# Seven block products in place of eight for two pairs of token-layer chunks, and an older setup in place of a halved one

## The chip, the cores and the metric

The kernel runs on one core of a Trainium2 chip. A core has a TensorE (PE, matrix products; PEld is its weight load), a VectorE (DVE), a ScalarE (ACT), a GpSimd (POOL) and a SyncE (SP, which here only issues transfers); they run side by side and wait for one another at semaphores. Products land in PSUM, eight banks of 128 partitions by 512 float32; everything else lives in SBUF. The metric is the device time of one execution in microseconds (us). Each instruction has one of these engines, and each engine works through its own list in the order in which the program issued it: an instruction that waits holds up all that stand behind it on its engine.

## The reference, cut to what matters

For each of 8 batches a 3008 x 256 input goes through a two-dimensional Fourier transform, of which the real part x is kept, and then through an MLP mixer block: a token layer across the 3008 positions and a channel layer across the 256 channels.

```python
X = np.fft.fft(x, axis=1)
x = np.fft.fft(X, axis=2).real

xt = x.transpose(0, 2, 1)                       # batch, 256, 3008
h = np.maximum(xt @ w_tok1, 0.0) @ w_tok2       # 3008 -> 256 -> 3008
u = x + h.transpose(0, 2, 1)
h2 = np.maximum(u @ w_ch1, 0.0) @ w_ch2         # 256 -> 1536 -> 256
return u + h2
```

The step that the change is about is the second token product, `max(.., 0) @ w_tok2`, and the sum with x that follows it.

## The kernel before

A batch is computed in six chunks of 512 positions (the last has 448 of its own). A chunk is computed in four steps, so that a batch has 24 steps, s0 to s23. A step does a quarter of the first channel product of its chunk (`mm1`, six matmuls of 512 columns into three banks `pc`, each emptied by ACT), a quarter of the second channel product of the chunk before it (`mm2`), and between these it takes pieces from generators that prepare the next batch. The channel product is itself computed with block sums on VectorE (`block_sums`, tiles `sb` and `c`), seven products for eight.

```python
for b in range(BB):
    nxt = front(b + 1) if b + 1 < BB else iter(())
    if b != 1:
        folds = fold(b + 2, [nc.vector] * 4) if b + 2 < BB else None
    for c in range(NCH):
        ...
        for s in range(4):
            sub = 4 * c + s
            n = plan[b][sub]
            mm1(b, c, c1, range(3 * s, 3 * s + 3))
            ...                                    # now(): half of the block sums
            take(own, own_plan[b][sub])            # the rest of this batch's front
            first = 0 if s % 2 else n // 2
            take(nxt, first)                       # pieces of the next batch's front
            ...
            if prev is not None:
                mm2(*prev, s, pbox)
            ...
            take(nxt, n - first)
            ...
            if folds is not None:
                take(folds, fold_plan[b][sub])     # pieces of the fold of batch b + 2
            ...
            if b and sub == 22 and b + 3 < BB:
                x_tiles[b + 3] = load_x(b + 3)     # one buffer: waits for the fold's end
```

`load_x` brings a batch's input (`xp` by four plain transfers, `xm` by two gathers, all issued by GpSimd) into single buffers. `fold` adds the mirrored rows of `xm` to `xp` on VectorE (a mirror piece) and then forms sums and differences of columns in `eo` (two more pieces), four times:

```python
for s, (t0, t1) in enumerate(((13, 17), (9, 13), (5, 9), (1, 5))):
    ...
    if s == 0:
        tt(out=xp[:, 1:NR, 0], in0=xp[:, 1:NR, 0], in1=xm[0:KR, ::-1, 0], op=add)
        tt(out=eo[:, :, 0], in0=xp[:, :, 0], in1=xp[:, :, 0], op=add)
    tt(out=xp[:, t, 1:D], in0=xp[:, t, 1:D], in1=xm[0:KR, rv, D - 1:0:-1], op=add)
    yield
    ...                                            # eo sums; yield; eo differences; yield
fold_plan = [[0] * 8 + [1, 2, 0, 0] * 4 for _ in range(BB)]      # from s8 on
```

`front(b)` makes the transform of a batch (tiles `z`, `w`), the first token product (`pt`), the upper half of x (`third(c)`: `pq` and `py` into PSUM, `yt` on VectorE) and then, chunk by chunk, the second token product with the sum:

```python
def third(c, then=None):
    py, pq = ps_f("py"), ps_f("pq")
    ...                                            # 4 + 4 matmuls of 128 columns
    nc.scalar.activation(out=qs[:], in_=pq[:], func=AFT.Copy)
    ...
    for h, op in ((0, AT.subtract), (1, AT.add)):
        nc.vector.tensor_tensor(out=yt[:, h, CW * c:CW * c + CW], in0=py[:],
                                in1=qs[:], op=op)
...
for c in range(NCH):
    ...
    for h in range(2):
        minus = c >= 3
        pu = ps_f("pu")
        for th in range(2):
            nc.tensor.matmul(pu[:, 0:n], lhsT=uu[:, th, int(minus), h, :],
                             rhs=w2_cols(b, c)[:, th], start=(th == 0), stop=(th == 1))
        ...
        nc.vector.tensor_tensor(out=ut[:, h, 0:n]..., in0=pu[:, 0:n]..., in1=y..., op=AT.add)
        ...
        yield
```

So a chunk takes four matmuls of 512 columns and two adds of 128 x 512 on VectorE. The three banks `ps_f` rotate among `pz`, `pw`, `pt1`, `py`, `pq` and `pu`.

Setup builds tables from angles. Its middle part works in two halves of the groups, so that ScalarE may start on the first half while VectorE makes the second:

```python
for g in halves:
    nc.vector.scalar_tensor_tensor(out=mp[:, g], ...)
for g in halves:
    for i, scale, bias in ((mp, 1.0 / S, up), (vp, 1.0, down)):
        nc.scalar.activation(out=vp[:, g], in_=i[:, g], func=AFT.Identity, ...)
rest_of(halves[0])
...
for g in halves:
    table3(tp, vp, g)
...
warm(12)
pts_p = turn_in(tp, ps_mm)
turned_out(tts_p, pts_p, (0,))
angles_z()
turned_out(tts_p, pts_p, (1,))
table_q()
...
```

Of the kernel before, what the change touches and what calls it, by code (L numbers as in the profile page):

```python
# [10 lines left out]
FP16 = mybir.dt.float16  # L11
# [9 lines left out]
P = 128  # L21
# [20 lines left out]
def kernel(  # L42
# [30 lines left out]
    def ps_f(name, dt=FP32, n=512):  # L73
        return psum.tile([P, n], dt, tag="f", name=name, bufs=3)
# [6 lines left out]
    def ps_any(name, dt=FP32, n=512):  # L81
        tag, bufs = next(r for r in ring if r[0] not in held)
        return psum.tile([P, n], dt, tag=tag, name=name, bufs=bufs)
# [103 lines left out]
    ts(eq32[:], scol[:], 32.0, AT.is_equal)  # L187
    nc.vector.scalar_tensor_tensor(out=reff[:], in0=gt32[:], scalar=-32.0, in1=scol[:],
# [58 lines left out]
    def table3(tab, r, g, shift=(0.0, 0.0)):  # L247
        for i in range(2):
            nc.scalar.activation(out=tab[:, g, 64 * i:64 * i + 64], in_=r[:, g],
                                 func=AFT.Sin, scale=half[i][:], bias=shift[i])  # L250
# [16 lines left out]
    def turned_out(tts, pts, hs=(0, 1)):  # L267
        for h in hs:
            copy(0, tts[0][:, 768 * h:768 * h + 768], pts[h][:, 0:768])
# [46 lines left out]
    halves = slice(0, NG // 2), slice(NG // 2, NG)  # L316
    for g in halves:
        nc.vector.scalar_tensor_tensor(
            out=mp[:, g], in0=jrow[:, 0:64].unsqueeze(1).to_broadcast([P, NG // 2, 64]),
            scalar=r47[:], in1=gp[:, g].unsqueeze(2).to_broadcast([P, NG // 2, 64]),  # L320
            op0=AT.mult, op1=AT.add)
    ts(mid[:], scol[:], 32.0, AT.is_lt)
    ts(tmp[:], scol[:], 1.0, AT.is_ge)
    nc.vector.tensor_tensor(out=mid[:], in0=mid[:], in1=tmp[:], op=AT.mult)
# [4 lines left out]
    for g in halves:  # L329
        for i, scale, bias in ((mp, 1.0 / S, up), (vp, 1.0, down)):  # L330
            nc.scalar.activation(out=vp[:, g], in_=i[:, g], func=AFT.Identity,  # L331
                                 scale=scale, bias=bias[:])

    def rest_of(g):
        nc.vector.scalar_tensor_tensor(out=vp[:, g], in0=vp[:, g], scalar=-float(S),
                                       in1=mp[:, g], op0=AT.mult, op1=AT.add)

    rest_of(halves[0])
# [3 lines left out]
    rest_of(halves[1])  # L342
    ident = const.tile([P, P], FP16, tag="ident")
    ts(ident[:], jrow[:, 0:P], pcol[:], AT.is_equal)
# [6 lines left out]
    for g in halves:  # L351
        table3(tp, vp, g)
    anti = const.tile([P, P], FP16, tag="anti")
    acol = pvec("acol")

    def table_q():
        for g in halves:
            nc.vector.scalar_tensor_tensor(out=vq[:, g], in0=vp[:, g], scalar=side[:],
                                           in1=vp[:, g], op0=AT.mult, op1=AT.max)
        for g in halves:  # L360
            table3(tq, vq, g, (shift0[:], shift1[:]))

    def table_anti():
        ts(acol[:], pcol[:], -1.0, AT.mult, 127.0, AT.add)
        ts(anti[:], jrow[:, 0:P], acol[:], AT.is_equal)

    mask0, mask0h, q24 = (pvec(n) for n in ("mask0", "mask0h", "q24"))
    t1n = const.tile([KR, 2, 2, 24], FP16, tag="t1n")
    t1b = const.tile([KR, 3, 24], FP16, tag="t1b")
    m1 = gen.tile([KR, 5, 24], FP32, tag="m1")  # L370
    cs, v1 = (gen.tile([KR, 5, 24], FP32, tag=n, name=n) for n in ("cs", "v1"))
    t0h = gen.tile([KR, 2, 24], FP16, tag="t0h")

    def angles_z():
        ts(mask0h[:], xicol[:], -0.5, AT.mult, 0.5, AT.add)
        ts(q24[:], qcol[:], 24.0, AT.add)
        for a, n, col, off in ((0, 2, qcol, 47 / 4), (2, 2, qcol, 0.0),
                               (4, 1, q24, 47 / 8)):
            ts(m1[:, a:a + n, :], jrow[0:KR, 0:24].unsqueeze(1).to_broadcast([KR, n, 24]),
               col[0:KR, :], AT.mult, off, AT.add)  # L380
        reduced(v1[:], m1[:], m1[:], 47)
        sin(cs[:], m1[:], 47)
        nc.scalar.activation(out=t0h[:], in_=cs[:, 0:4:2, :], func=AFT.Copy,
                             scale=mask0h[0:KR, :])

    def table_z():
        ts(mask0[:], mask0h[:], 2.0, AT.mult)
        for i, m in ((0, mask0), (1, xicol)):
            ts(t1n[:, :, i, :], cs[:, i:4:2, :], m[0:KR, :], AT.mult)
        ts(t1b[:, 1, :], cs[:, 4, :], float(np.sqrt(0.5)), AT.mult,  # L390
           xicol[0:KR, :], AT.mult)
        nc.vector.tensor_copy(out=t1b[:, 0:3:2, :], in_=t1n[:, :, 0, :])

    nyq = const.tile([KR, P], FP16, tag="nyq")
    ixc = const.tile([P, 1], I32, tag="ixc")

    def rows_c():
        iota(ixc[:], [[0, 1]], D, -1)
        pl.memset(ixc[0:1, :], P)
        load_wc()  # L400

    def angles_d():
        nc.vector.scalar_tensor_tensor(out=md[:], in0=vd[:], scalar=-256.0, in1=md[:],
                                       op0=AT.mult, op1=AT.add)

    td0 = const.tile([P, 131], FP16, tag="td0")
    td1 = const.tile([P, P], FP16, tag="td1")
    alt = const.tile([P, 131], FP16, tag="alt")

# [57 lines left out]

    state = {}

    def fold(b, engs):  # L470
# [4 lines left out]
        for s, (t0, t1) in enumerate(((13, 17), (9, 13), (5, 9), (1, 5))):  # L475
            tt = engs[s].tensor_tensor
            t = slice(t0, t1)
            rv = slice(16 - t0, 16 - t1 if t1 < 17 else None, -1)
            if s == 0:
                tt(out=xp[:, 1:NR, 0], in0=xp[:, 1:NR, 0], in1=xm[0:KR, ::-1, 0], op=add)  # L480
                tt(out=eo[:, :, 0], in0=xp[:, :, 0], in1=xp[:, :, 0], op=add)
            tt(out=xp[:, t, 1:D], in0=xp[:, t, 1:D], in1=xm[0:KR, rv, D - 1:0:-1], op=add)
            yield
            if t0 == 1:
                t = slice(0, t1)
            tt(out=eo[:, t, 1:129], in0=xp[:, t, 1:129], in1=xp[:, t, 255:127:-1], op=add)
            if t0 == 1:
                nc.vector.tensor_copy(out=nyq[:, 0:1], in_=eo[:, 0, P:P + 1])
                nc.vector.memset(eo[:, 0, P:P + 1], 0.0)
            yield  # L490
            tt(out=eo[:, t, 129:256], in0=xp[:, t, 1:128], in1=xp[:, t, 255:128:-1],
               op=sub)
            yield
# [92 lines left out]
    Z0_ORDER = ((11, (0, 1)), (0, (1, 1)), (6, (0, 1)), (1, (0, 1)))  # L586
# [37 lines left out]
    def rest(b):  # L624
# [11 lines left out]
        def part_q(pt):  # L636
            sq = perb.tile([P, 127], FP32, tag="sq", name="sq", bufs=2)
            nc.scalar.activation(out=sq[:], in_=pt[:, 130:257], func=AFT.Copy)
            return sq

        def units(pt, sq):
            uv = perb.tile([P, 2, P], FP32, tag="uv", name="uv", bufs=2)
            nc.vector.tensor_copy(out=uv[:, :, 0], in_=pt[:, 0:130:129])
            nc.vector.tensor_tensor(out=uv[:, 0, 1:P], in0=pt[:, 2:129], in1=sq[:],
                                    op=AT.subtract)
            nc.vector.tensor_tensor(out=uv[:, 1, 1:P], in0=pt[:, 2:129], in1=sq[:],
                                    op=AT.add)
# [11 lines left out]
        def third(c, then=None):  # L659
            py, pq = ps_f("py"), ps_f("pq")  # L660
# [5 lines left out]
            qs = perb.tile([P, CW], FP32, tag="qs", name="qs", bufs=2)  # L666
# [21 lines left out]
        else:  # L688
# [3 lines left out]
            for th in range(2):  # L692
                pt = ps_mm("pt1")
                tok1(pt, th, 0)
                sp = perb.tile([P, 130], FP32, tag="sp", name="sp", bufs=2)
# [17 lines left out]
        uts = st["ut"] = []  # L713
        for c in range(NCH):
            if c in (1, 2):
# [4 lines left out]
            ut = perb.tile([P, 2, CW], FP16, tag="ut", name="ut", bufs=4)  # L720
# [4 lines left out]
            uts.append(ut)  # L725
# [19 lines left out]
            for h in range(2):  # L745
# [6 lines left out]
                if minus:  # L752
                    hi = 2 * HALF - 1 - f0
                    y = yt[:, 1 - h, hi:hi - n:-1]
                else:
                    y = yt[:, h, f0:f0 + n]
# [3 lines left out]
                    in1=y.rearrange("p (a b) -> p a b", b=64), op=AT.add)  # L760
# [192 lines left out]
    warm(12)  # L953
    held.add("o2")
    pts_p = turn_in(tp, ps_mm)
    turned_out(tts_p, pts_p, (0,))
    angles_z()
    turned_out(tts_p, pts_p, (1,))
    table_q()
    table_anti()  # L960
    table_z()
    filler(6)
    turn_rows(tts_p, 1.0, 0)
    filler(10)
    pts_q = turn_in(tq, ps_out)
    filler(4)
    rows_c()
    pieces = fold0()
    take(pieces, 2)
    angles_d()  # L970
    take(pieces, 3)
    own = zw0()
    take(own, 2)
    turned_out(tts_q, pts_q, (0,))
    take(own, 3)
    turned_out(tts_q, pts_q, (1,))
    held.clear()
    take(own, 3)
    table_d()
    table_b()  # L980
    carried(tts_p, hp, 0, 0)
    carried(tts_p, hp, 1, 1)
    turn_rows(tts_q, -1.0, 0)
    carried(tts_p, hp, 2, 1)
    table_perm()
    take(own, 7)
# [18 lines left out]
    for c in range(2, NCH):  # L1005
        for th in range(2):
# [7 lines left out]
    plan = [[0] * 10 + [2] * 10 + [1, 2, 2, 3]] + [[1] * 14 + [2, 1] * 4 + [1, 1]] * (BB - 1)  # L1014
    own_plan = [[2, 1, 1, 1, 1, 1, 1, 0, 1, 1, 0, 0, 1, 1] + [0] * 10,
                [0, 1, 1, 0, 1, 1, 1, 0, 1, 1, 0, 0, 1, 1] + [0] * 10]
    own_plan += [[1, 1, 1, 0, 0, 1, 1, 0, 1, 1, 0, 0, 1, 1] + [0] * 10] * (BB - 2)
    early_plan = [0] * 4 + [2, 2, 1, 2, 1, 2, 2] + [0] * 13
    fold_plan = [[0] * 8 + [1, 2, 0, 0] * 4 for _ in range(BB)]
# [5 lines left out]
    for b in range(BB):  # L1025
# [3 lines left out]
        for c in range(NCH):  # L1029
# [6 lines left out]
            for s in range(4):  # L1036
                sub = 4 * c + s
                n = plan[b][sub]
# [77 lines left out]
```

## Time and profile before

| | before |
|---|---|
| time, median of three | 595.34 us (594.62 to 595.8) |
| span of the profiled execution | 592.8 us |
| first channel product of batch 0 starts | 32.30 us |
| PE, DVE, ACT, POOL busy | 579.1, 459.5, 438.5, 153.2 us |
| adds `ut<-pu,yt` on VectorE | 94, mean 674 ns |
| loads of `xp` and `xm` | 8 of each batch's, 6 issues each |

The span counts from the first to the last instruction. "Busy" is the time in which an engine has at least one instruction in work, so that the sum over the rows of an engine can be more than its busy time: on VectorE one instruction begins before the one ahead has quite ended. In a timeline a line is a run of like instructions: its start, its length, the engine, the line of the kernel, output and inputs. "Idle before" names what ended an engine's wait. The clock granted to PE is full in every slice.

### The profile page before, as it was taken

What the parts mean: (1) busy time and instruction counts of PE and PEld (TensorE: products, weight loads), DVE (VectorE), ACT (ScalarE), POOL (GpSimd) and SP (SyncE); (2) the same over time, 40 slices, a digit from 0 to 9 for tenths busy, and PEclk for the clock granted to TensorE, in tenths of its full rate; (3) what the DMA queues carried; (4) which work ended last, traced back from release to release, by engine and by line L of the source; (5) the groups of instructions that cost most, each with busy time, mean ns of one, the idle gap of its engine ahead of it and who ended that gap; (6) DMA issues with size and microseconds to landing.
All of it is one profiled execution on the core that took longest, in us unless ns stands there. A gap on an engine that the chain in (4) does not pass through costs nothing.

```text
span 592.8 us, 15951 instructions
## 1 busy us (share of the span) xinstructions
PE 579.1 (98%) x6389; PEld 418.7 (71%) x6389; DVE 459.5 (78%) x1076; ACT 438.5 (74%) x999; POOL 153.2 (26%) x253
## 2 busy tenths in 40 slices
PE   4999999999999999999999999999999999999997
PEld 3846777767776777676777667767777767766675
DVE  8868689978896887769797787868888777676572
ACT  8775887887778777777768777787777877766772
POOL 7630421412151211421134111511221121112131
PEclk9999999999999999999999999999999999999999
DMA  9995861863467242844329432492233335334324
GB/s 152 210 187 128 129 108 44 155 119 54 67 122 137 55 89 56 156 71 98 64 48 170 98 65 55 91 171 54 56 81 64 73 55 98 47 72 77 78 61 101
DMA packets 86682, 56.55 MB, mean 95 GB/s; under 512 B 54944, under 2 KB 83552, under 8 KB 85856
## 3 DMA queue, kind: packets, MB, share of 16 engines
q1 hardware_dynamic: 77984, 37.77, 33.5%
q0 software_dynamic: 8320, 17.49, 17.2%
q8 instruction: 50, 0.82, 0.6%
q10 hardware_dynamic: 304, 0.26, 0.2%
q14 instruction: 24, 0.20, 0.1%
HBM read 34.98 MB, written 24.64 MB: 101 GB/s over the span
## 4 chain that ended last, share of the span: by engine, by line
PE 96%; DVE 3%; ACT 0%; issue 0%; POOL 0%; DVEq 0%; POOLq 0%
PE pc L792 41%; PE px L836 25%; PE py L836 10%; PE pu L749 7%; PE pt L632 4%; PE po L907 2%; PE pz L537 2%; PE pq L664 1%; PE py L664 1%; PE py L855 1%; PE pw L615 1%; PE pw L616 1%; PE pw L579 1%; DVE z L302 0%; DVE xp L507 0%; ACT vp L331 0%
## 5 line engine op out<-in xcount | busy, mean ns | idle before, releaser
L795 ACT ACTIVATE c<-pc 128x512 f16<-128x512 f32 (+1 forms) x574 | 297.9, 595 | 31.0 <-PE pc L792 16.1
L818 POOL TENSOR_TENSOR osb<-osb,rt 128x256 f32<-128x256 f32 (+1 forms) x92 | 84.2, 915 | 375.5 <-DVE osb L818 368.3
L836 PEld LDWEIGHTS <-c 128*128 128x128 f16 x2112 | 128.1, 98 | 24.8
L792 PE MATMUL pc<-ut,wc1p 128*128 128x512 f16 x576 | 140.0, 379 | 0.5 <-DVE ut L302 0.5
L792 PE MATMUL pc<-ut,wc1m 128*128 128x512 f16 (+1 forms) x576 | 134.9, 370 | 0.0
L841 ACT ACTIVATE m<-px 128x256 f32<-128x256 f32 (+1 forms) x138 | 51.8, 375 | 75.1 <-PE px L836 42.2
L836 PEld LDWEIGHTS <-sb 128*128 128x128 f16 x1584 | 94.5, 98 | 10.4
L757 DVE TENSOR_TENSOR ut<-pu,yt 128x512 f16<-128x512 f32 (+1 forms) x94 | 63.3, 674 | 40.2 <-PE pu L749 40.1
L792 PEld LDWEIGHTS <-wc1p 128*128 128x128 f16 x576 | 52.0, 97 | 49.2 <-DMA wc1p<-in_moe_w_ch_dram,ixc 0.8
L792 PEld LDWEIGHTS <-wc1m 128*128 128x128 f16 x576 | 52.9, 98 | 45.0
L836 PE MATMUL px<-wst,c 128*128 128x128 f16 x1056 | 74.0, 219 | 0.0
L836 PE MATMUL px<-wc,c 128*128 128x128 f16 x1056 | 66.5, 219 | 0.0
L818 DVE TENSOR_TENSOR osb<-py,m 128x256 f32<-128x256 f32 (+1 forms) x92 | 37.5, 407 | 26.5 <-ACT m L841 26.2
L809 DVE TENSOR_TENSOR sb<-sb,c 128x768 f16<-128x768 f16 (+1 forms) x92 | 55.0, 598 | 3.2
L749 PE MATMUL pu<-w2p,uu 128*128 128x512 f16 (+1 forms) x184 | 54.7, 379 | 0.0
L809 DVE TENSOR_TENSOR c<-c 128x768 f16<-128x768 f16 (+1 forms) x92 | 51.0, 554 | 0.0
L809 DVE TENSOR_TENSOR sb<-c 128x768 f16<-128x768 f16 (+1 forms) x92 | 50.6, 550 | 0.0
L809 DVE TENSOR_TENSOR sb<-c,sb 128x768 f16<-128x768 f16 (+1 forms) x92 | 49.9, 543 | 0.0
L304 ACT ACTIVATE z<-pz 128x480 f16<-128x480 f32 (+1 forms) x59 | 38.7, 667 | 5.5 <-PE pz L546 3.0
L618 DVE SCALAR_TENSOR_TENSOR w<-alt,pw 128x131 f16<-128x131 f16 x84 | 29.2, 350 | 16.4 <-ACT w L304 15.9
L671 DVE TENSOR_TENSOR yt<-py,qs 128x512 f16<-128x512 f32 x48 | 30.9, 685 | 10.3 <-ACT qs L667 10.2
L836 PE MATMUL py<-wst,sb 128*128 128x128 f16 x528 | 37.1, 219 | 0.0
(200 smaller groups left out, 648.1 us busy)
## 6 DMA issues: line engine op xcount, KB each, us to landing
out_dram<-osb SPq DMA_DIRECT2D x83, 256.0 KB, 3.5
xp<-in_x_dram POOLq DMA_DIRECT2D x16, 272.0 KB
out_dram<-osb SPq DMA_DIRECT2D x11, 192.0 KB, 3.2
xp<-in_x_dram POOLq DMA_DIRECT2D x16, 127.5 KB
rt<-ut SPq DMA_TRANSPOSE x96, 3.8
w2s<-in_moe_w_tok_dram POOLq DMA_DIRECT2D x1, 1504.0 KB
w1p<-in_moe_w_tok_dram POOLq DMA_DIRECT2D x4, 192.0 KB
wc<-in_moe_w_ch_dram POOLq DMA_DIRECT2D x1, 768.0 KB
```

Source lines behind the costliest of these rows:

```text
L304: nc.scalar.activation(out=out_, in_=in_, func=AFT.Copy)
L618: nc.vector.scalar_tensor_tensor(out=w[:, g, 0:131], in0=alt[:], scalar=pw[:, 131:132], in1=pw[:, 0:131], op0=AT.mult, op1=AT.add)
L632: nc.tensor.matmul(pt[:, o:o + n], lhsT=hw[:, g, th * P:th * P + P], rhs=w[:, g, f:f + n], start=(g == 0), stop=(g == NG - 1))
L671: nc.vector.tensor_tensor(out=yt[:, h, CW * c:CW * c + CW], in0=py[:], in1=qs[:], op=op)
L749: nc.tensor.matmul(pu[:, 0:n], lhsT=uu[:, th, int(minus), h, :], rhs=w2_cols(b, c)[:, th], start=(th == 0), stop=(th == 1))
L757: nc.vector.tensor_tensor(out=ut[:, h, 0:n].rearrange("p (a b) -> p a b", b=64), in0=pu[:, 0:n].rearrange("p (b a) -> p a b", b=64), in1=y ...
L792: nc.tensor.matmul(pc[:, 0:n], lhsT=wc[:, h, ct * P:(ct + 1) * P], rhs=ut[:, h, 0:n], start=(h == 0), stop=(h == 1))
L795: nc.scalar.activation(out=c1[:, ct, 0:n], in_=pc[:, 0:n], func=AFT.Relu)
L809: nc.vector.tensor_tensor(out=o, in0=x, in1=y, op=op)
L818: eng.tensor_tensor(out=o, in0=x, in1=y, op=AT.add)
L836: nc.tensor.matmul(o[:, t], lhsT=a(k)[:, f:f + P], rhs=w(k), start=(first and t == 0 and k == 0), stop=(k == HC - 1), skip_group_check=True)
L841: nc.scalar.activation(out=m[:, i, t1], in_=pa[:, 0], func=AFT.Copy)
```

## The change

It does two things. In the batches from the third on, the chunk pairs 0-1 and 3-4 of the second token product are computed with seven block products in place of eight (a product of 2 x 2 blocks: rows are the two halves `h` of the channels, the middle is the two halves `th` of the 256 hidden tokens, columns are the two chunks). The sums of weight blocks are made once, in batch 1, by GpSimd, and lie in the room of the raw `w2s`; the sums of the left blocks are made in each batch by VectorE (`usum`). It is for TensorE: seven matmuls of 512 columns for eight in each pair. And the setup is the one without halves, an earlier state of the kernel. Around these the plans that spread the pieces over the 24 steps are written anew.

```diff
+    PAIRS = (0, 3)
+    wsum = w2f[:, 0:4096].rearrange("p (i j s) -> p i j s", i=2, j=4)
+    usum = w2f[:, 4096:5120].rearrange("p (j m s) -> p j m s", j=4, m=2)
+    def w2_sums():
+        for i, c in enumerate(PAIRS):
+            ...
+            for o, x, y in ((t1, b12, b11), (t2, b22, t1), (t3, b22, b12), (t4, b21, t2)):
+                pl.tensor_tensor(out=o, in0=x, in1=y, op=AT.subtract)
+                yield
 ... (fold)
+        if b >= 4:                       # from batch 4 on: all four mirror pieces first
+            for s, (t, rv) in enumerate(parts):
+                mirror(s, t, rv)
+                yield
 ... (rest of front, b > 1)
+        def pair_u(c):
+            m, i = int(c >= 3), PAIRS.index(c)
+            pa, px, pb = ps_f("pa", hold=True), ps_f("pu"), ps_f("pb", hold=True)
+            ...
+            mm(pa, uu[:, 0, m, 0, :], wa[:, 0], True)
+            t0 = part()
+            plus(t0, pa, add_y(0, c), "v")
+            yield
+            mm(px, uu[:, 1, m, 0, :], wa[:, 1], True)
+            plus(into(ua, 0), px, t0)
+            yield
+            mm(pb, usum[:, 0, m, :], wsum[:, i, 0, :], True)
+            mm(pa, usum[:, 1, m, :], wsum[:, i, 1, :])
+            t1 = part()
+            plus(t1, pa, add_y(0, c + 1), "v")
+            yield
+            mm(pa, usum[:, 2, m, :], wsum[:, i, 2, :])
+            t2 = part()
+            plus(t2, pa, add_y(1, c + 1), "v")
+            plus(into(ub, 1), pb, t2)
+            yield
+            mm(pa, uu[:, 1, m, 1, :], wsum[:, i, 3, :])
+            plus(into(ua, 1), pa, add_y(1, c))
+            yield
+            mm(pb, usum[:, 3, m, :], wb[:, 1])
+            plus(into(ub, 0), pb, t1)
+            yield
+        if b > 1:
+            ...                          # usum: four sums of 128 x 256 on VectorE
+            third(1)
+            yield
+            yield from pair_u(0)
+            third(2)
+            yield
 ... (setup)
-    for g in halves:                     # mp, near, rest_of, table3 in two halves
+    nc.vector.scalar_tensor_tensor(out=mp[:], ...)      # whole tiles
+    near(vp, mp)
 ...
-    warm(12)
+    warm(24)
+    table3(tq, vq, (shift0[:], shift1[:]))
 ...
-    turned_out(tts_q, pts_q, (0,))
+    take(own, 3)
+    table_b()
+    take(own, 3)
+    turned_out(tts_q, pts_q)
 ... (plans)
-    plan = [...] + [[1] * 14 + [2, 1] * 4 + [1, 1]] * (BB - 1)
+    plan += [list(zip([0, 0, 1, 0, 0, 0, 0, 0, 1, 0, 0, 1, 0, 2, 0, 0, 1, 2, 1, 0, 1, 0, 0, 0],
+                      [2, 1, 2, 2, 0, 1, 0, 1, 2, 1, 1, 2, 2, 0, 0, 2, 0, 0, 0, 0, 1, 1, 2, 1]))] * (BB - 2)
+    sums_plan = [0, 1, 1, 2, 0, 0, 1, 1, 1, 0, 1, 0, ...]
-    fold_plan = [[0] * 8 + [1, 2, 0, 0] * 4 for _ in range(BB)]
+    fold_plan = [[0, 1, 0, 0, 1, 0, 0, 0, 2, 1, 0, 0, 3, 0, 0, 0, 0, 2, 0, 0, 2, 0, 0, 0] for _ in range(BB)]
```

`pa` and `pb` are held through a pair (`hold=True`): of the three `ps_f` banks only one is left for others meanwhile, and the five matmuls into `pa` go one after the other onto what is there, with a read by VectorE between each two. In the order of the instructions, the pair 0-1 of a batch from the fourth on stands at steps s17 to s21 of the batch before it, the pair 3-4 at s4 to s8 of its own batch; for the third batch the pair 0-1 stands at s16 to s19 of batch 1. The first mirror piece of a fold, which needs the whole of a load, stands at s1 (it stood at s8); the last piece of a fold stands at s20 (it stood at s21), and the load of the next input still at s22. Batch 1 keeps its fold plan.

## The prediction, made before the changed kernel was run

> **What bounds the kernel now.** I read the shares of busy time first, then the chain that ended last, then TensorE's waits, and last the stretches of single batches.
>
> ```profile
> span 592.8 us, 15951 instructions
> PE 579.1 (98%) x6389; PEld 418.7 (71%) x6389; DVE 459.5 (78%) x1076; ACT 438.5 (74%) x999; POOL 153.2 (26%) x253
> ...
> PE 96%; DVE 3%; ACT 0%; issue 0%; POOL 0%; DVEq 0%; POOLq 0%
> ...
> L792 PE MATMUL pc<-ut,wc1p 128*128 128x512 f16 x576 | 140.0, 379 | 0.5 <-DVE ut L302 0.5
> L757 DVE TENSOR_TENSOR ut<-pu,yt 128x512 f16<-128x512 f32 (+1 forms) x94 | 63.3, 674 | 40.2 <-PE pu L749 40.1
> L749 PE MATMUL pu<-w2p,uu 128*128 128x512 f16 (+1 forms) x184 | 54.7, 379 | 0.0
> ```
>
> The chain is TensorE's for 96%, and the two matmul rows have next to no idle time before them. The stretches of batches 2 and 3 (170.4 to 241.0 us and on) say it outright: TensorE is busy for the whole of each, and VectorE for 56.47 of 70.60 us, 80%.
>
> ```profile
> 170.40:241.00 70.60, 70.60 (x806) 51.38 (x804) 56.47 (x129) 52.90 (x122) 17.82 (x28) 1.00 0.47 91
> 241.00:310.70 69.70, 69.70 (x776) 50.34 (x775) 55.35 (x129) 52.62 (x122) 16.93 (x28) 1.00 0.46 91
> ```
>
> So from 32.3 us to about 588 us a TensorE microsecond saved is one gained, but a wait put into TensorE's list is one lost in full: there is no slack to hide it in. Setup (the first 32 us) is another regime: TensorE idles 6.1 us at the start, and ACT and VectorE set the pace to about 21 us.
>
> The last thing to see is a load of a batch's input. GpSimd waits for the end of the fold that reads the old data, issues six transfers, and the traffic then runs near 200 GB/s until it breaks off:
>
> ```profile
> 308.81 2.12 POOL L163 DMA_DIRECT2D xp<-in_x_dram  x4 [4.64 <-DVE eo L491]
> 311.23 1.06 POOL L153 DMA_INDIRECT xm<-in_x_dram,ix  x1 [0.30 <-issue]
> 312.60 0.94 POOL L153 DMA_INDIRECT xm<-in_x_dram,ix  x1 [0.30 <-issue]
> ...
> 320.00:322.00 2.00, 2.00 (x23) 1.40 (x22) 1.78 (x4) 2.00 (x5) 0.00 (x0) 1.00 2.41 244
> 322.00:323.00 1.00, 1.00 (x18) 0.84 (x16) 1.00 (x4) 0.43 (x2) 0.00 (x0) 1.00 0.06 6
> ```
>
> The first three lines are the timeline of GpSimd, the last two are stretches with the GB/s at the end. From the first issue to the break are 322.0 - 308.8 = 13.2 us; the same reading of three other loads gives 12.6, 12.6 and 13.3 us. In the kernel before nothing waits for this: the load lands about 11 us into a batch (batch 4 begins at 310.76), and its first user, the mirror piece at s8, stands some 22 us into it.
>
> **What the Trainium skill says.** "TensorE: Matmul & The Clock Gate", section "Back-to-back issue gap", gives 216 ns for an isolated matmul of 512 columns and 131 ns in a sustained stream. The trace agrees with the first: six of them in 1.29 to 1.30 us of the chain, 0.216 us each. "VectorE: DVE Perf Modes", section "The perf-mode tier table", has two-tensor operations with a PSUM operand at one element per cycle, those on 16-bit SBUF data at two. The trace agrees: 128 x 512 from PSUM takes 0.68 us, 128 x 768 of f16 in SBUF 0.54 to 0.60 us. "Perfetto Trace Analysis", section "Optimizing Tensor Performance", asks that independent groups rotate through banks, so that emptying one overlaps the matmuls of the next. The change gives that up inside a pair: five matmuls go to one bank with reads between. No page bears on the loads as they are used here.
>
> **The change part by part.**
>
> 1. *Matmuls removed.* Two pairs in each of batches 2 to 7 lose one 512-column matmul: 12 x 0.216 = **-2.6 us**, all on the path.
>
> 2. *VectorE work added.* A pair has seven adds of 128 x 512 for four, so six more per batch, about 0.62 us each (0.68 less the 0.07 by which neighbours overlap), 3.7 us; and four `usum` sums of 128 x 256 f16, 0.2 us each. That is 4.5 us on 56, 60.1 of some 69 us: 87%. It fits on average; what counts is where it is crowded. I went through steps s15 to s23 by hand, each engine in its order with the durations above. In batch 1, where the front of batch 2 is done in a hurry, the second `third` follows the first without a step between (its fourth bank waits for ACT's copy, 0.4 us), a matmul into `pa` waits for VectorE's read in s18 (0.45 us), and a product into `py` in s23 waits for its bank (0.2 us): **+1.0 us**. In batches 2 to 6 `third(1)` at s16 puts the block sums behind two adds that wait for ACT, so that `mm2` of s17 may wait about 0.4 us: 5 x 0.4, which I halve as the margin is as small as my error: **+1.0 us**. The spacing of the pair's own pieces, a step each, covers the rest of its waits: a read is done 1 to 2 us before the next matmul into that bank.
>
> 3. *The mirror piece at s1.* It needs the whole load, and VectorE takes its list in order. For batches 3 to 5: the fold now ends in s20, by my account 5.3 us before the batch begins (it was 1.95 before). So the load lands at -5.3 + 13.0 = +7.7 us; VectorE arrives at the piece at about +6.5 us, waits 1.2 us, and needs 1.5 us for it. TensorE first needs what stands behind it in s3, the emptied half of `py`, at +9.7 (odd batch) to +10.4 us (even), and VectorE has that ready at +9.5. So 0 to 1.5 us each, **+1.5 us** for the three. For batch 2 the load is issued in batch 1, whose fold still ends in s21 and behind a VectorE that lags by 3 us: issue at -1.3, landing at +11.6, the piece done at +13.1, `py` free at +13.5; TensorE would need it at +10.4. **+3.2 us**, once.
>
> 4. *Setup.* Whole tiles in place of halves: `mp` (768 elements per partition) ends at about 5.2 us where its first half ended at 4.6; ACT makes the two steps of `vp` by 7.2, then waits for the angles of `z` on VectorE (done 8.35), and the rest of `vp` ends at 9.3. The first table is ready at 11.1 us where it was 9.1. But the fold of batch 0 starts at 12.6 us in both, and the first `pw` product needs `z`, which I get at 19.2 us by ACT's list (19.0 before). `tts_q` is then 0.8 us later than it was, with TensorE bound from there on: **+0.8 us**.
>
> 5. *GpSimd's 16 sums* in batch 1: they lie beside other work, since GpSimd is 26% busy and waits 4.9 us for the fold ahead of the load there. Nothing.
>
> Sum: -2.6 + 1.0 + 1.0 + 1.5 + 3.2 + 0.8 = +4.9 us, 600.2 us.
>
> **The rivals.** (a) *All new waits are absorbed*, VectorE's 13% of slack is enough, and the setups tie: only the matmuls count, 592.7 to 593.5 us. For it speaks that VectorE waits 40.1 us for `pu` in the kernel before, so that it is mostly ahead of TensorE, and that the plans are plainly fitted to something. Against it: those waits are gone where the new adds stand, and a fixed order does not lend slack to other steps. (b) *The load is slower, or VectorE becomes the bound behind it*: if a load lands 15 us after its issue (one reading, with stores between, had 14.8), each of four batches waits some 2 us more, and VectorE at 87% needs eight steps to catch up, with waits at every block sum: 606 to 612 us. For it: 0.87 busy leaves a lag of 3 us to be made up in 23 us. Against: 13.2 us or less in four of five loads. (c) *Setup alone decides*: ACT's list is 2 us later at the first table, and if that comes through whole, +1.2 us more, 601 us.
>
> **Range and chances.** I give (a) a third, my sum and (c) together rather more than half, (b) a tenth. The mean is near **598 us**; 592.5 (rival a, whole) to 604.5 (my sum and the lower part of b) should hold it 8 times in 10. Faster by 2% is under 583.4 us: it would need 12 us, and the removed matmuls are worth 2.6; 0.01. Slower by 2% is over 607.2 us: the upper part of (b), 0.04. Within 2%: 0.95. Of the sign I am less sure than of the size: slower, about 3 to 1.
>
> **What would show it.** Step 1: 172 matmuls of the second token product in place of 184 (`pu`, `pa`, `pb` together), and less TensorE busy time by 2.6 us in the main part. Step 2: VectorE busy about 60 of 69 us in a batch, and waits of TensorE for `tc` or `sb` of 0.2 to 0.5 us in s17 and s18. Step 3: VectorE waiting for the load ahead of the first mirror piece, 5 us or more in batch 2 and 1 us in batches 3 to 5, and a TensorE wait of about 3 us in s3 of batch 2 for an `osb` add. Step 4: the first channel product at 33.1 us in place of 32.3. I am wrong if TensorE has no wait in batch 2 (then the load landed sooner or its reader did not hold what I think), if VectorE's list keeps ahead in s16 to s18, or if setup differs by more than 2 us either way.

## The result, and the profile after

| | before | after |
|---|---|---|
| time, median of four | 595.38 us (594.62 to 595.8) | 602.92 us (601.81 to 605.44) |
| ratio | | 1.0134, 95% interval 1.010 to 1.0168 |
| span of the profiled execution | 592.8 us | 603.6 us |
| first channel product of batch 0 starts | 32.30 us | 33.38 us |

The change costs 7.5 us. The profiled execution is the slowest of the four, some 11 us over the profiled one of before. First the head of the profile of the changed kernel.

```profile
span 603.6 us, 15998 instructions
PE 582.8 (97%) x6385; PEld 419.6 (70%) x6385; DVE 487.3 (81%) x1135; ACT 438.8 (73%) x994; POOL 167.0 (28%) x259
```

TensorE has less to do and is busy for longer: from the first channel product on 558.6 us in place of 556.3 (the rest of the difference lies in the setup). That already says that some of its work ran slowly. TensorE's waits, as total, number and longest one, are few, and the first two are new: products of the channel layer (`px`, `py`) wait for VectorE to empty a bank (`osb`), which cost 0.0 us before.

```profile
PE px L931 <- DVE osb L913: 3.2, 6, 1.9
PE py L931 <- DVE osb L913: 2.3, 1, 2.3
PE ph L439 <- DMA w1m<-in_moe_w_tok_dram: 1.0, 1, 1.0
...
PE pa L751 <- DVE tc L760: 0.3, 1, 0.3
```

Two single waits of about 2 us stand out, and a third of 1.0 us belongs to the setup. Cutting the trace at the first channel product of each batch places them:

| | setup | b0 | b1 | b2 | b3 | b4 | b5 | b6 | b7 to the end |
|---|---|---|---|---|---|---|---|---|---|
| before, us | 32.30 | 68.37 | 69.63 | 70.66 | 69.64 | 70.66 | 69.64 | 70.66 | 71.28 |
| after, us | 33.38 | 68.36 | 76.31 | 73.56 | 70.17 | 70.91 | 70.17 | 70.87 | 69.85 |

Batch 1 gives 6.7 us, batch 2 gives 2.9. About 1 us of batch 1 is only work moved: it has 786 matmuls where it had 776, and batch 7, which is 1.4 us shorter, has 690 for 703. The stretches of batches 1 to 3 of the changed kernel (columns: length, then busy time of PE, PEld, DVE, ACT, POOL, granted clock, share of the DMA engines, GB/s):

```profile
101.74:178.05 76.31, 73.32 (x786) 51.75 (x785) 68.35 (x149) 53.03 (x123) 28.88 (x38) 0.98 0.43 83
178.05:251.61 73.56, 70.85 (x803) 51.33 (x802) 59.32 (x138) 53.06 (x122) 21.04 (x31) 1.00 0.52 96
251.61:321.78 70.17, 69.72 (x774) 50.18 (x772) 59.05 (x138) 52.74 (x122) 17.17 (x28) 1.00 0.47 90
```

Batch 1 has TensorE idle for 3.0 us and a mean clock under 1. Three places explain the table.

**Batch 1, s4 to s6.** The timelines of VectorE, GpSimd and TensorE in the changed kernel, one fence each:

```profile
117.24 3.22 DVE L904 TENSOR_TENSOR sb<-sb,c 128x768 f16<-128x768 f16 x1
120.38 0.41 DVE L913 TENSOR_TENSOR osb<-px,m 128x256 f32<-128x256 f32 x1
```

```profile
116.72 1.01 POOL L913 TENSOR_TENSOR osb<-osb,rt 128x256 f32<-128x256 f32 x1
117.70 1.19 POOL L469 TENSOR_TENSOR w2s<-w2p 128x512 f16<-128x512 f16 x1
118.85 1.19 POOL L469 TENSOR_TENSOR w2s<-w2p,w2s 128x512 f16<-128x512 f16 x1
120.00 0.52 POOL L908 COPY rt<-rt 128x4 f16<-128x4 f16 x1
```

```profile
118.07 0.83 PE L931 MATMUL py<-wst,sb 128*128 128x128 f16 x12
120.84 0.83 PE L931 MATMUL px<-wst,sb 128*128 128x128 f16 x12 [1.95 <-DVE osb L913]
...
121.94 2.38 PE L887 MATMUL pc<-ut,wc1p 128*128 128x512 f16 x6
```

A VectorE block sum that takes 0.56 us elsewhere lasts 3.22 us: it ends 0.4 us after GpSimd's unbroken run of an add and two weight sums does (120.04 us). The `osb` add stands behind it in VectorE's list, and TensorE waits 1.95 us for that. Then six matmuls take 2.38 us that take 1.46 elsewhere. The stretches show why, cut where the clock changes: the granted clock (the third number from the end) is 0.50 from 122.33 to 125.74 us, and 1.00 before and after.

```profile
118.91:122.33 3.42, 1.49 (x24) 1.29 (x24) 3.29 (x4) 0.88 (x3) 3.06 (x4) 1.00 1.03 174
122.33:125.74 3.41, 3.41 (x15) 1.68 (x14) 0.53 (x1) 2.37 (x5) 0.92 (x1) 0.50 1.18 204
```

3.41 us at half the clock are 1.7 us lost, nearly as much as the wait itself.

**Batch 2, s3.** The load, its reader on VectorE and TensorE's wait:

```profile
176.81 2.12 POOL L170 DMA_DIRECT2D xp<-in_x_dram  x4 [4.27 <-DVE eo L506]
```

```profile
190.19 0.23 DVE L483 TENSOR_TENSOR xp<-xp,xm 94x16 f16<-94x16 f16 x1 [6.40 <-DMA xm<-in_x_dram,ix]
...
190.90 0.41 DVE L913 TENSOR_TENSOR osb<-py,m 128x256 f32<-128x256 f32 x1
```

```profile
191.37 0.83 PE L931 MATMUL py<-wc,sb 128*128 128x128 f16 x12 [2.34 <-DVE osb L913]
```

This is the wait of the prediction's step 3: 190.19 - 176.81 = 13.4 us from issue to use, VectorE idle for 6.40 of them, TensorE for 2.34.

**Batches 2 to 6, s17.** VectorE and then TensorE:

```profile
231.99 1.29 DVE L685 TENSOR_TENSOR yt<-py,qs 128x512 f16<-128x512 f32 x2 [0.43 <-ACT qs L681]
233.19 0.55 DVE L904 TENSOR_TENSOR sb<-c 128x768 f16<-128x768 f16 x1
233.78 0.56 DVE L904 TENSOR_TENSOR sb<-sb,c 128x768 f16<-128x768 f16 x1
234.25 0.42 DVE L913 TENSOR_TENSOR osb<-px,m 128x256 f32<-128x256 f32 x1
```

```profile
234.72 0.83 PE L931 MATMUL px<-wst,sb 128*128 128x128 f16 x12 [0.25 <-DVE osb L913]
```

The two adds of `third(1)` wait for ACT, the block sums stand behind them, and TensorE is late by some 0.5 us (0.25 shown as a wait; the run of products before it, 0.94 us in place of 0.83, is held up too).

### The profile page after: what moved, and what is told of

Read it like the earlier page. It is cut to its first block, busy times and chain, and to the rows that moved or that the text cites. A ratio compares the mean times of both kernels' runs of the same rounds, so it can differ in the third digit from the quotient of the medians.

```text
span 603.6 us, 15998 instructions
## 1 busy us (share of the span) xinstructions
PE 582.8 (97%) x6385; PEld 419.6 (70%) x6385; DVE 487.3 (81%) x1135; ACT 438.8 (73%) x994; POOL 167.0 (28%) x259
## 5 line engine op out<-in xcount | busy, mean ns | idle before, releaser
L913 POOL TENSOR_TENSOR osb<-osb,rt 128x256 f32<-128x256 f32 (+1 forms) x92 | 85.9, 934 | 381.9 <-DVE osb L913 369.5
L904 DVE TENSOR_TENSOR sb<-c 128x768 f16<-128x768 f16 (+1 forms) x92 | 56.0, 608 | 0.0
L904 DVE TENSOR_TENSOR sb<-c,sb 128x768 f16<-128x768 f16 (+1 forms) x92 | 51.9, 564 | 0.0
L931 PE MATMUL px<-wst,sb 128*128 128x128 f16 x528 | 37.0, 219 | 3.2 <-DVE osb L913 3.2
L931 PE MATMUL py<-wc,sb 128*128 128x128 f16 x528 | 37.0, 219 | 2.3 <-DVE osb L913 2.3
L314 ACT ACTIVATE z<-pz 128x480 f16<-128x480 f32 (+1 forms) x60 | 37.2, 726 | 2.6 <-PE pz L561 1.7
L852 DVE TENSOR_TENSOR ut<-pu,yt 128x512 f16<-128x512 f32 (+1 forms) x46 | 29.9, 658 | 8.8 <-PE pu L849 8.6
```

The lines of the kernel that those rows point to most:

```text
L314: nc.scalar.activation(out=out_, in_=in_, func=AFT.Copy)
L852: nc.vector.tensor_tensor(out=ut[:, h, 0:n].rearrange("p (a b) -> p a b", b=64), in0=pu[:, 0:n].rearrange("p (b a) -> p a b", b=64), in1=a ...
L904: nc.vector.tensor_tensor(out=o, in0=x, in1=y, op=op)
L913: eng.tensor_tensor(out=o, in0=x, in1=y, op=AT.add)
L931: nc.tensor.matmul(o[:, t], lhsT=a(k)[:, f:f + P], rhs=w(k), start=(first and t == 0 and k == 0), stop=(k == HC - 1), skip_group_check=True)
```

## The experiments

The theory after this reading: four causes, GpSimd's sums in batch 1, the load, the order in s16, and 1.1 us of setup. The rivals are named run by run. Every ratio is against the kernel before, run beside it (594.8 to 595.0 us; 595.38 beside the changed kernel).

| run | time, us | ratio, 95% interval |
|---|---|---|
| changed kernel | 602.92 | 1.0134 (1.010 to 1.0168) |
| without the sums | 598.88 | 1.0072 (1.005 to 1.0093) |
| mirror piece at s5 | 599.65 | 1.0085 (1.0063 to 1.0106) |
| block sums first in s16 | 598.69 | 1.0057 (1.004 to 1.0074) |
| setup in halves | 602.95 | 1.0131 (1.0103 to 1.016) |
| sums later, one per step | 599.93 | 1.0098 (1.007 to 1.0127) |
| kernel before, with the sums | 597.15 | 1.0042 (1.0029 to 1.0054) |
| sums on VectorE | 599.72 | 1.0086 (1.0069 to 1.0103) |
| three edits at once | 596.33 | 1.0023 (1.0014 to 1.0032) |
| kernel before, sums in one run | 599.69 | 1.0077 (1.0061 to 1.0092) |
| best, halved setup | 594.67 | 0.9999 (0.999 to 1.0007) |
| best, whole setup | 594.17 | 0.9990 (0.9983 to 0.9997) |
| best, fold earlier | 595.61 | 1.0013 (1.0006 to 1.0019) |

### 1. Without GpSimd's sums

```diff
                 if b == 1:
-                    take(w2_parts, sums_plan[sub])
+                    pass
```

The weight sums are left out, so the seven products use what stands in that room; only the time is of use.

> The changed kernel without GpSimd's eight weight-block sums in batch 1 (the block products then use raw weights; everything else is as it was). Theory 'GpSimd keeps VectorE from SBUF': the 3.2 us block sum on VectorE in s5 of batch 1 falls back to 0.56 us, TensorE's wait of 1.95 us there and the clock dip after it go, and the time falls by about 4.5 us, to 598.4. Rival 'the gathers and the traffic of the load issued at 112 us do it': the wait stays, 602.5 to 603.3.

4.0 us less. In the trace batch 1 falls from 76.31 to 72.19 us, and the block sum at the same place is short again:

```profile
115.73 0.56 DVE L904 TENSOR_TENSOR sb<-sb,c 128x768 f16<-128x768 f16 x1
```

The wait in s5 is gone and the clock stays at 1.00, while the load that was the rival is still there. The sums are the cause: of 4.1 us in batch 1 some 2.4 are waits and 1.7 are the lower clock.

### 2. The first mirror piece at s5

```diff
-    fold_plan = [[0, 1, 0, 0, 1, 0, 0, 0, 2, 1, ...
+    fold_plan = [[0, 0, 0, 0, 1, 1, 0, 0, 2, 1, ...
```

> The changed kernel with the first mirror piece of the fold at s5 instead of s1 in batches 2 to 5. Theory 'VectorE stands behind the load': TensorE's wait of 2.3 us in s3 of batch 2 and the 0.37 us in s3 of batches 3 and 5 go, 3.3 to 3.6 us less, 599.4. Rival 'VectorE is so full that a moved piece moves the wait': under 1 us less, 602 to 603, with new waits in s5 to s9.

Batch 2 goes from 73.56 to 70.73 us, 2.8 less. Batches 3 and 5 stay at 70.16: nothing was lost to the load there. The wait of batch 2 is not the same in every execution: the time from issue to use was 13.4 us in the changed kernel's trace, and 12.9, 12.0, 11.9, 11.5 and 11.3 us in five other runs whose piece stands at s1 (runs 1, 3, 4, 5 and 7), with losses around s3 of 2.8 down to 0.7 us, 1.6 on average of the six. The median fell by 3.3 us, more than the load accounts for. A reason may be the clock: the profiled execution had the same 1.94 us wait in s5 of batch 1, but no lower clock behind it:

```profile
115.67:119.09 3.42, 2.00 (x19) 1.20 (x17) 3.39 (x2) 1.96 (x4) 3.42 (x4) 1.00 0.96 166
119.09:122.50 3.41, 2.89 (x32) 1.94 (x32) 1.88 (x4) 2.02 (x5) 2.57 (x3) 1.00 1.11 232
```

These stretches are cut at multiples of 3.41 us from the trace's first change of clock. Here the wait is spread over two of them (1.41 and 0.53 us of idle time); in the changed kernel it lay in one (1.93 us, from 118.91 to 122.33). The last section comes back to this.

### 3. Block sums of s16 ahead of the adds

```diff
-                if s == 3:
+                if s == 3 or (b and sub == 16):
                     now()
 ...
-                if s == 0:
+                if s == 0 and not (b and sub == 16):
                     now()
```

> The changed kernel with the two block sums of s16 ahead of the third(1) adds on VectorE in batches 1 to 7. Theory 'the sums are late because they stand behind two adds that wait for ACT': the 0.54 us that s17 loses in each of batches 2 to 6 go, 2.2 to 2.7 us less, 600.4. Rival 'ACT is what s17 waits for in the end, through the kept copy m': no more than 0.5 us less, 602.4 to 603.

VectorE now has the sums done before ACT's copy is there, and its wait is gone:

```profile
230.90 0.55 DVE L904 TENSOR_TENSOR sb<-c 128x768 f16<-128x768 f16 x1
231.49 0.56 DVE L904 TENSOR_TENSOR sb<-sb,c 128x768 f16<-128x768 f16 x1
231.96 1.28 DVE L685 TENSOR_TENSOR yt<-py,qs 128x512 f16<-128x512 f32 x2
233.16 0.41 DVE L913 TENSOR_TENSOR osb<-px,m 128x256 f32<-128x256 f32 x1
```

Batches 3 to 6 take 69.65, 70.38, 69.66 and 70.35 us: 0.5 less each; with s17 of batch 2 (3.07 us in place of 3.58) 2.6 for the five. The median fell by 4.2, again more than that. Four of its five executions had a mean clock of 1.000 (598.0 to 598.8 us); the fifth, the profiled one, had 0.997, half a clock for 3.41 us in batch 1, and 602.3 us. So the lower clock comes and goes between executions of one kernel, and medians of four executions carry 1 to 2 us of such luck. Sizes below are therefore taken from batch lengths.

### 4. The setup in halves

The changed kernel with the setup of the kernel before (whole tiles back to group halves, `warm(24)` to `warm(12)`).

> The changed kernel with the setup of the kernel before (in halves). Theory 'setup costs what the first channel product is late by': 1.1 us less, 601.8, the first channel product back at 32.3 us. Rivals: the late setup was hidden by later waits (no change, 602.9), or the old setup also shifts loads of batch 0 and 1 (2 us or more).

No change: 602.95. In nine profiles with the whole setup batch 0 starts at 32.16 to 33.38 us, 32.74 on average; in five with the halved one at 32.27 to 32.30 four times and at 32.98 once, 32.43 on average. In the changed kernel's trace the difference is TensorE's 1.0 us wait for the load of `w1m`. On average the setup is worth 0.3 us, less than its own scatter, and the 1.1 us of the table are mostly that one execution.

### 5. The same sums, one per step

```diff
-    sums_plan = [0, 1, 1, 2, 0, 0, 1, 1, 1, 0, 1, 0, 0, 0, ...
+    sums_plan = [0, 0, 0, 0, 0, 0, 1, 1, 1, 1, 1, 1, 1, 1, ...
```

> The changed kernel with its eight GpSimd weight sums moved: one per step in s6 to s13 of batch 1, in place of one or two per step in s1 to s10. The number of sums and their cost on GpSimd stay. Theory (GpSimd in a run of back-to-back tensor operations keeps a 16-bit VectorE operation waiting until the run ends: 0.56 us became 3.22): single sums 2.9 us apart block one VectorE operation for at most one sum, about 1.2 us, which VectorE's slack takes up. The stretched sum of 3.22 us, TensorE's 1.95 us wait in s5 and the lower clock after it go, batch 1 ends up near the 72.2 us that it has with the sums left out, and the time falls by 3 to 4.5 us, to 598.5 to 600. Rival (the amount of GpSimd work counts, wherever it stands): the wait turns up in other steps of batch 1 and the time stays within 1 us of 602.9.

3.0 us less, with the same number of sums. Batch 1 is 73.33 us long, 1.15 over the run without sums: VectorE operations beside a sum take 0.9 to 1.5 us, and TensorE has small losses in s11, s13, s15 and s18. The sums do not stay a step apart: GpSimd does three back to back from 128.2 us on and two from 141.6, but no VectorE operation is held over more than one of them. Most of the cost lies in the place, a part in the sums.

### 6. The sums in the kernel before

The eight sums are added to the kernel before, at the same steps, into a tile that nothing reads; no product changes.

> The kernel BEFORE with the eight GpSimd weight sums of the changed kernel added at the same steps of batch 1, into a tile that nothing reads; all products stay as they were. Theory (the sums alone cause the loss in batch 1): batch 1 grows from 69.6 us by 2 to 4.5 us, one VectorE block sum takes over 2 us in s4 or s5, and the time is 597 to 599.5 against 595.0. Rival (the sums only hurt because the changed plan already crowds VectorE in batch 1): the time stays within 0.7 us of 595.0, though single VectorE operations are stretched.

2.35 us more, and batch 1 is 71.57 us long for 69.63. VectorE and GpSimd in that run:

```profile
117.88 3.42 DVE L825 TENSOR_TENSOR c<-c 128x768 f16<-128x768 f16 x1
```

```profile
117.77 1.20 POOL L481 TENSOR_TENSOR w2s<-w2p,w2s 128x512 f16<-128x512 f16 x1
118.91 0.19 POOL L829 COPY rt<-rt 128x4 f16<-128x4 f16 x1
119.06 0.66 POOL L834 TENSOR_TENSOR osb<-osb,rt 128x256 f32<-128x256 f32 x1
119.69 1.19 POOL L481 TENSOR_TENSOR w2s<-w2p 128x512 f16<-128x512 f16 x1
```

The sums alone bring a 3.42 us block sum, held over four GpSimd operations. The cost is 1.9 us in place of 4.1: TensorE loses some 0.8 us each in s3 and s6, with no lower clock.

### 7. The sums on VectorE

```diff
-                pl.tensor_tensor(out=o, in0=x, in1=y, op=AT.subtract)
+                nc.vector.tensor_tensor(out=o, in0=x, in1=y, op=AT.subtract)
```

> The changed kernel with the eight weight sums on VectorE in place of GpSimd, in the same steps. It adds 8 x about 0.5 us to VectorE in s1 to s10 of batch 1 and takes 8 x 1.2 us from GpSimd. Theory (blocking of VectorE by GpSimd is what costs): the stretched operations go, VectorE's own 4 us are mostly within its slack, and the time is 599 to 600.5. Rival (VectorE has no slack in s1 to s5 of batch 1, so any work that reaches it is paid): 4 us of VectorE time come through and the time stays at 602 to 603.

Batch 1 takes 72.19 us, the same as with no sums at all. On VectorE a sum takes 0.42 us:

```profile
111.64 0.42 DVE L469 TENSOR_TENSOR w2s<-w2p,w2s 128x512 f16<-128x512 f16 x1
```

Eight of them are 3.4 us that fall into its slack. GpSimd, which had three quarters of its time free in the kernel before, was the dearer place.

### 8. Three edits at once

Runs 2, 3 and 5 together.

> The changed kernel with three edits at once: first mirror piece at s5 (batches 2 to 5), block sums ahead of the adds in s16, GpSimd's sums one per step in s6 to s13 of batch 1. The setup stays the changed one. Theory (three separate causes, which add): of the loss of 10.8 us of the profiled span go about 4 (sums and the lower clock behind them), 2.8 (load) and 2.5 (s17), and what is left over is 1.5 us or so against a gain of 2.6 in matmuls: 592.5 to 595, about the kernel before or a little under. Rival (they share a part, such as the lower clock, so that each alone already takes most of it): 596 to 598.

596.33 is at the lower edge of the rival. The batches say that the causes add: batch 2 loses 2.9 us of its length, batches 3 to 6 lose 0.5 each, batch 1 loses 3.0. What the expectation left out is what batch 1 keeps: 73.33 us, with losses in s3, s11, s13, s15 and s18.

### 9. All eight sums in one run

The kernel before with the sums of run 6, all in s12 of batch 1. It decides how long a VectorE operation is held.

> The kernel BEFORE with the same eight GpSimd weight sums, all eight in one run in s12 of batch 1 (about 9.6 us of GpSimd without a pause), into a tile that nothing reads. Theory (a 16-bit VectorE operation that starts inside a run of GpSimd operations gets through only when the run ends): one VectorE operation takes 5 to 9 us, TensorE waits 4 to 7 us behind it, batch 1 grows by 4 to 8 us, time 599 to 604. Rival (VectorE gets its turn between two GpSimd operations, so that one operation is held for 1.2 us at most, and the 3.22 us of the changed kernel was an accident of order): several operations of 1.5 to 1.9 us, VectorE some 5 us later in sum, batch 1 longer by 1 to 3 us, time 596 to 598.

VectorE and GpSimd in the middle of it:

```profile
142.73 1.41 DVE L498 TENSOR_TENSOR xp<-xp,xm 94x1020 f16<-94x1020 f16 x1
144.17 1.31 DVE L502 TENSOR_TENSOR eo<-xp 94x512 f16<-94x512 f16 x1
145.40 0.34 DVE L634 SCALAR_TENSOR_TENSOR w<-alt,pw 128x131 f16<-128x131 f16 x1
145.66 0.41 DVE L834 TENSOR_TENSOR osb<-py,m 128x256 f32<-128x256 f32 x1
...
147.11 1.44 DVE L825 TENSOR_TENSOR sb<-sb,c 128x768 f16<-128x768 f16 x1
```

```profile
142.09 1.51 POOL L481 TENSOR_TENSOR w2s<-w2p 128x512 f16<-128x512 f16 x1
143.55 1.64 POOL L481 TENSOR_TENSOR w2s<-w2p,w2s 128x512 f16<-128x512 f16 x1
145.16 1.50 POOL L481 TENSOR_TENSOR w2s<-w2p 128x512 f16<-128x512 f16 x1
```

My theory falls in its strong form: nothing is held for the whole run. The two engines take turns: each VectorE operation on two SBUF tensors gets through after one sum, and takes 1.0 to 1.55 us in place of 0.4 to 0.7; each sum takes 1.4 to 1.6 us in place of 1.2. Operations with a PSUM input (`osb<-py,m` 0.41 us, `w<-alt,pw` 0.34 us) pass untouched. Eight such turns put VectorE far enough behind for two waits of TensorE, 1.27 and 3.39 us, and batch 1 is 6.4 us longer. About 1.5 us of that is the clock again, 0.50 from 151.43 to 154.84 us; the other three executions had a mean clock of 1.000. The size was that of the theory (599 to 604), the mechanism that of the rival.

"SBUF — State Buffer", section "Who interferes with whom", in the Trainium skill says that VectorE operations with both inputs in SBUF and GpSimd operations that read SBUF exclude each other, the second one blocked until the first has finished. This run agrees. The operations of 3.22 and 3.42 us do not: they were held over three and four GpSimd operations in a row. The 3.22 recurs in four profiled kernels with that order of work (the changed one and runs 2 to 4), so it is no accident of one execution. In both the run of GpSimd operations holds an `osb` add among the sums, in run 9 sums alone, but an `osb` add by itself made no block sum longer than 1.52 us in the kernel before; why VectorE misses its turn there and gets it here stays open.

### 10 and 11. The best version found

```diff
-                pl.tensor_tensor(out=o, ...)                  # sums on VectorE
+                nc.vector.tensor_tensor(out=o, ...)
 ... (mirror piece at s5, block sums of s16 first: as in runs 2 and 3)
-    plan += [...]                # batch 1: third0, usum, third1 in s15, the pair from s16
+    plan += [...]                # batch 1: third0, usum in s15, third1 in s16, the pair from s17
+    for b in (3, 5):                                          # z pieces a step later
+        plan[b] = plan[b][:2] + [(1, 1), (0, 3)] + plan[b][4:]
```

The second half of batch 1 now has the plan of the later batches, and one of the `z` pieces of s2 moves to s3, there and in batches 3 and 5. Run 10 has the halved setup, run 11 the whole one.

> The changed kernel with everything that the runs so far found: weight sums on VectorE, first mirror piece at s5, block sums of s16 ahead of the adds, batch 1 with the second half of the plan of the later batches (third(1) in s16, the pair's first piece in s17), the last z pieces of batches 3 and 5 one step later (s3), and the setup in group halves as in the kernel before. Theory (the waits are separate and the removed matmuls come through once the waits are gone): batch 1 near 71.0 us, batches 2 to 6 at 69.4 to 70.4, time 592 to 593.5, 1.5 to 3 us under the kernel before. Rival (each wait that is taken away uncovers the next, so that the order of work has no place for seven products): 594.5 to 596.5.

> As the run before it, with the changed kernel's setup of whole tiles. In five profiled runs so far this setup started the first channel product between 32.16 and 33.38 us, the halved one at 32.27 to 32.30. Theory (the setup's own work ties and what differs is a wait for a weight load that comes and goes): 0 to 0.7 us over the run before it. Rival (whole tiles cost their 0.8 us): 0.7 to 1.2 us over it.

594.67 and 594.17 us. The second is 0.7 us under the kernel before, with an interval that just excludes equality. So the setup ties (run 11 is even 0.5 us faster), and the seven products come out about even: 0.1% ahead with the whole setup, level with the halved one. Batches 1 to 3 of run 11:

```profile
101.24:172.31 71.07, 70.90 (x787) 51.08 (x786) 65.93 (x155) 52.79 (x123) 19.16 (x31) 1.00 0.49 91
172.31:243.43 71.12, 70.38 (x803) 51.27 (x802) 61.42 (x140) 53.05 (x122) 20.66 (x30) 1.00 0.54 97
243.43:312.92 69.49, 69.39 (x773) 50.09 (x772) 58.90 (x138) 52.67 (x122) 17.28 (x28) 1.00 0.48 91
```

Batch 3 is 0.15 us shorter than before the change, batch 4 (70.39) 0.27; batch 2 has a new loss of 0.9 us in s0, behind a VectorE that is busy 65.93 of 71.07 us in batch 1. The rival, that each wait removed uncovers the next, was half right.

### 12. The fold of batch 1 earlier

```diff
-    fold_plan[1] = [3, 3] + [0] * 7 + [2] + [0, 0, 1, 2, 0, 0, 1, 2, 0, 0, 2, 2, 0, 0]
+    fold_plan[1] = [3, 3] + [0] * 7 + [2] + [0, 0, 1, 2, 1, 2, 0, 2, 0, 2, 0, 0, 0, 0]
```

> The best version so far with whole setup, and in batch 1 the last five pieces of the fold on VectorE one to three steps earlier (s14, s15, s17, s19 in place of s16, s17, s20, s21). In the run before, VectorE had no idle time from s17 of batch 1 to s1 of batch 2, and TensorE waited 0.74 us there behind an osb add, after a loss of 0.9 us in s22. Theory (VectorE is only crowded at the end of batch 1, and has 1.0 us of room in s14 and 0.5 us in s15): both losses go, batch 1 falls from 71.07 to about 70.2 us, batch 2 from 71.12 to 70.4, and the time is 592.5 to 593.3. Rival (VectorE is full over the whole second half of batch 1, so the wait only moves forward to s15 to s18): 593.7 to 595.

A miss: 595.61 us. Batch 2 gets its 0.8 us back (70.35), batch 1 loses 2.2 (73.30). TensorE's two new waits:

```profile
156.45 0.83 PE L931 MATMUL px<-wst,sb 128*128 128x128 f16 x12 [0.90 <-DVE osb L913]
165.93 0.38 PE L751 MATMUL pa<-w2s,uu 128*128 128x512 f16 x1 [0.92 <-DVE tc L760]
```

The fold piece moved into s15 stands ahead of the block sums, and the wait only moves forward, as the rival has it, though the time is above its 593.7 to 595. Its reason holds in part: in run 11 VectorE is busy for 7.24 of the 9 us from 144 us on (s14 to s16), and for 15.96 of the 16.3 us from 156 us to the end of the batch. The loss that the expectation saw in s22 was none: s22 takes 2.68 us here too, as it does in the batches after it.

## Why the prediction was right or wrong

The time of 602.92 us lies in the range, and "slower, by less than 2%" was right. The sum of 600.2 us was nearer than the 598.0 us that I gave after mixing in the rivals, and it was made of a missing term and some that partly offset it; that the time still lies in the range is partly luck.

- **Step 5, GpSimd's sums: "Nothing". This is the step that failed.** The sums cost 4.0 us (run 1), by holding VectorE's block sum in s5 (3.22 us in place of 0.56), for which TensorE waits. I read GpSimd's 26% busy as room, and did not ask what else its operations hold up. They are also eight and not the 16 that I wrote; the error made no difference, as I gave them nothing. The kernel before had a sign of it: a block sum there takes 1.40 us beside a GpSimd residual add (at 323.8 us).
- **Step 2, VectorE crowded.** The mechanism was right and one size was off. VectorE came to 59.05 of 70.17 us in batch 3, for 60.1 of 69 (4.5 on 56 would be 60.5). Batch 1: 1.0 predicted; of its three places two are in the trace at the size worked out, 0.40 us lost ahead of `py` in s15 and 0.45 ahead of `pa` in s18, and the one in s23 is not; putting the plan of the later batches there, with one `z` piece moved, gave 1.1 (72.19 to 71.07). s17 of five batches: I worked out 0.4 each and halved it "as the margin is as small as my error"; it was 0.51 to 0.53 each, 2.6 in all for 1.0. The halving was the mistake: this wait follows from the order of VectorE's list, and it came in all five batches alike.
- **Step 3, the mirror piece.** Batch 2: 3.2 predicted, 2.8 in the trace, by the chain I described, though 0.7 to 2.8 from run to run. Batches 3 to 5: 1.5 predicted, nothing measured; VectorE waits 0.65 and 0.86 us for the load in batches 3 and 4 and not at all in 5, and TensorE does not notice. What was mis-sized is the load: I had it 13.0 us long, and here it is in use 11.9, 11.3 and 11.3 us after its issue. My reading of 13.2 us took the end of all traffic for the end of the load: its own queue had moved all of its 384 packets (1.60 MB) by 10.9 us, and what followed were SyncE's transposes `rt<-ut`.
- **Step 1, matmuls.** 172 products as counted (88 in `pu`, 84 in the pairs). The -2.6 us are only partly seen, and TensorE's busy time in the main part rose by 2.4 us where I wanted it 2.6 lower. With the waits removed (run 11), batches 3 and 4 gain 0.15 and 0.27 of the 0.43 us each; small losses of 0.30 us in s4 of batch 3 and 0.17 in s0 of batch 4 are about the rest.
- **Step 4, setup.** 0.8 predicted, at 33.1 us; the trace had 33.38, which looked like agreement and was not: the halved setup in the same kernel changed nothing (run 4).
- **The rivals.** (a) was wrong about the waits; even run 11, with most of them gone, stays above its 592.7 to 593.5. (b) was wrong: the load took 13.4 us or less, and VectorE, at 59.05 of 70.17 us in batch 3, did not become the bound behind it. (c) was wrong: the halved setup gains nothing (run 4).

The terms of the profiled execution, from batch lengths: 4.1 (sums, 1.7 of it lower clock), 2.8 (load), 2.6 (s17), 1.1 (batch 1) and 1.1 (setup) are 11.7 us. Its span grew by 10.7 (603.58 - 592.84), so that 1.0 of the 2.6 us for the removed matmuls came through. With the averages over the profiles for the load (1.6) and the setup (0.3) the sum is 8.7 us, or 7.0 in an execution without the lower clock; the medians differ by 7.5.

## What to carry to other kernels

An idle engine is not a free one: before work is moved to GpSimd, ask which VectorE operations read two SBUF tensors at that time, and whether the next one in TensorE's order stands behind them; here 3.4 us on a crowded VectorE cost nothing, and the same sums on a free GpSimd cost 4, or 1.2 where they stood later and further apart (run 5). Where TensorE is busy 98%, a saving of 0.2 us per product is soon eaten by the waits that a new order brings (0.25 to 2.3 us here), so write the VectorE list of each step down in order and put what TensorE waits for first. Do not read a difference of 1 us from one trace: repeat the piece whose cause you name.

## What was unexpected of the hardware

- A VectorE operation on two f16 SBUF tensors beside GpSimd's tensor operations takes 0.9 to 1.5 us in place of 0.4 to 0.7 where it is held over one of them (runs 5 and 9), and 3.22 or 3.42 us where it is held over three or four.
- The clock granted to TensorE was 0.50 for one stretch of 3.41 us in the main part of four profiled executions (the changed kernel, runs 3, 4 and 9), which cost 1.5 to 1.7 us each. In all fourteen traces of this case the clock changes only at multiples of 3.41 us from its first change, and half the clock follows just those intervals in which TensorE was idle for 1.93 us or more; behind intervals with 1.68 us or less it stays full. So one and the same wait of 1.94 to 1.96 us was followed by half the clock where it fell into one interval (the changed kernel, runs 3 and 4) and not where a boundary cut it (run 2). The 2.34 us wait in batch 2 was cut as well, into 1.56 and 0.78 us, and had a full clock behind it. "TensorE: Matmul & The Clock Gate", section "What's actually happening", gives an activity window of about 3.4 us that runs free of the program, which fits, and would explain that the loss comes and goes. It asks for an idle window; here one that was idle for 57% of its length was enough. So such a wait costs up to about twice its own length, by where it falls.
